# Delta-rule attention with an expert layer: six half items by native fp32 products, and six weight splits put later

## The chip, the cores and the metric

The kernel runs on one core of one Trainium2 chip. The metric is the device time of one execution in microseconds (us); lower is better. All times below are in us unless marked ns.

## The reference

Four sequences with eight heads of width 48 run a delta rule over 768 steps; what comes out is the input of a two-layer network with 2048 hidden units. Everything is fp32.

```python
k_n = k / (norm(k) + 1e-06)
for t in range(S):                                     # S = 768
    y[:, :, t] = einsum('bhd,bhde->bhe', q[:, :, t], state)
    v_old = einsum('bhde,bhd->bhe', state, k_n[:, :, t])
    state = state + beta_t * einsum('bhd,bhe->bhde', k_n[:, :, t], v[:, :, t] - v_old)
x = y rearranged to 3072 tokens of 384
h = x @ w_in                                           # 384 x 2048
g = where(h >= 1, h, where(h <= -1, 0, (h + 1)**2 / 4))
out = g @ w_out                                        # 2048 x 384
```

## The kernel before, in words

**Attention.** The 768 steps are cut into 12 blocks of 64, and two blocks make a group G of 512 tokens. For a block, `gram_k` and `gram_q` (L233, L246) make products of its keys and queries, `lanes`, `solve` and `unlanes` invert a triangular matrix on VectorE (DVE), `merge16_a`, `merge16_b` and `merge32` (L391 to L444) join its parts with small products on TensorE (PE), and a chain through the state follows: `chain_r` (L446, state times keys), `chain_u` (L461), `chain_y` (L479, the block's output Y) and `chain_d` (L559, the new state). Each of them is a function that issues PE's products and returns its evictions from PSUM, which run on ScalarE (ACT) or DVE.

**The network.** It runs in items (G, f, blocks): the tokens of one or both blocks of a group against tile f of 16 weight tiles, each with 128 hidden units. `up` (L688) makes h; three activations on ACT (L812 twice, L844) and a maximum on DVE (L846) make g; `rest` (L803) splits g into a rounded part `ghi` on ACT (L807) and the remainder `glo` on DVE (L808); `down` (L697), two items behind, adds g times w_out to the sums `o`. PE multiplies fp32r, a rounded fp32. To keep precision each product is made of three passes over split operands (`PASSES`): high by high, high by low, low by high. So an item over one block (a half item, 256 tokens) has 9 matmuls in up and 6 in down; a whole item has 9 and 12, with 512 columns in up.

**Weights.** They lie in memory as 64-bit numbers and are unpacked in five steps for each tile f: `grow` (ACT, L191), `shift` (DVE, L197), `join` (DVE, L203), which makes the fp32 weight in X4, one of four places in the memory of `xb`; then the split, `cast` (ACT, L207) to the high part and `low` (DVE, L210) to the low part, both in `WT[f]`, which takes the memory of the raw tile `RAW[f]`. Y is split in the same way into `xb` when it is evicted, for block 0 by `direct` (L511: L515 on ACT, L520 on DVE).

**The order.** Nothing reorders the program: each engine takes its instructions as the code issues them, and an instruction that waits holds up those behind it on its engine. Group 0 begins with its only prologue, the front, where no Y is there yet. Its first six items (`HALF`) go over block 0 alone, as half items, while block 1 is still being solved; items 6 to 15 go over both blocks, and items 16 to 21 give the first six weight tiles to block 1. Around them, steps are put by hand. Tables of letters, FRONT for the front's stages and FILL for the items, say at which of six places in each item a step goes: A is the next step of ACT's list of grows and casts, D the next of DVE's list of shifts, joins and lows, F a filler, w a weight load, l another load, L a step of `lanes`, S of `solve`, U of `unlanes`, s, t, v and z scalings of V (L286), m and M masks of the query products (L266), B a copy of a Gram matrix (L611). PIECES says at which half item PE gets the pieces of block 1's chain: f6 are six fillers, a1 and b1 `merge16_a` and `merge16_b`, c1 and e1 the two parts of `merge32`, r1, u1, y1, d1 the chain, q2 the `gram_q` of block 2. Later groups are planned by the loops in `plan`, the same in both kernels.

**Fillers.** `dense(n)` issues n matmuls of 512 columns on a tile of zeros, whose results nobody reads; they occupy PE in the front while it has nothing to do. IDLE is the number of them after the fourth `gram_k`.

**Buffers.** h has two PSUM banks, `ch` two, o0 to o3 one each. The banks of h and o serve the chain too until the sums begin: `chain_d` of block 0 takes the two banks of h, which L576 on ACT empties. The const tiles `wt11` to `wt15` lend their memory to other things until their weights are loaded (`room`).

The order in which a step must follow another is told by this line in `plan`, which puts the chain of a group, with M = 14 items for group 0:

```python
for j, x in ((0, (0, None)), (0.5, (1, 0)), (2.5, (None, 1))):
    at(pe, G, M + j, lambda x=x: merge32(*x))
chain(G, M + 1.5, a)
```

So in item 14 PE has, in this order, up 14, a merge32 (L426), down 12, the next merge32, up 15, a `gram_k` (L239), down 13, `chain_u` (L467), up of tile 0 for block 1, and `chain_y` (L493). ACT evicts the merges (L441, L433, then L441 again, with copies L443), `gram_k` (L243) and `chain_u` (L476).

Of the kernel before, what the change touches and what calls it, by code (L numbers as in the profile page):

```python
# [22 lines left out]
IDLE = 18  # L23
DENSE = (8, 4, 8, 10)
HALF = 6
PASSES = ((0, 0), (0, 1), (1, 0))
# [14 lines left out]
def delta_rule_moe(ctx: ExitStack, tc: tile.TileContext, kqa, kqb, kv, beta, w, out):  # L41
# [157 lines left out]
    def join(f):  # L199
        x = X4[:, f % 4].bitcast(I32)  # L200
        if not PRELU:
            nc.vector.scalar_tensor_tensor(out=x, in0=RAW[f].bitcast(I32)[:, :, 1::2], scalar=-0x80000000, in1=x, op0=ALU.bitwise_and, op1=ALU.bitwise_or)
        nc.vector.scalar_tensor_tensor(out=x, in0=RAW.pop(f).bitcast(I32)[:, :, 0::2], scalar=29, in1=x, op0=ALU.logical_shift_right, op1=ALU.bitwise_or)  # L203

    def cast(f):
        WT[f] = const.tile([P, 2, 2, DM], F32R, name=f"wt{f}")
        nc.scalar.copy(out=WT[f][:, :, 0, :], in_=X4[:, f % 4])  # L207
# [13 lines left out]

    UNPACK = grow, shift, join, cast, low
# [256 lines left out]
    def chain_y(g):  # L479
        w_ = Q[g]  # L480
        if g % 2 == 0:
            XB[g // 2] = sb.tile([P, 2, 3, 2 * NB], F32R, name="xb")
        if g == 1:
            stg = const.tile([P, 2, 2 * DM], F32R, name=f"wt{FT - 1}")[:, :, 0:NB]
# [17 lines left out]
        if g == 0:  # L502
# [105 lines left out]

    def restore():
# [205 lines left out]
    for n, item in enumerate(items):  # L815
# [5 lines left out]
        if last:  # L821
            rest(*last)
# [4 lines left out]
        assert (item[1], low) in done, item  # L827
# [18 lines left out]
        nc.vector.tensor_tensor(out=s[:, c], in0=h[:, c], in1=s[:, c], op=ALU.max)  # L846
# [56 lines left out]
```

## Time and profile before

| what | value |
|---|---|
| median of 3 runs | 600.15 us (598.7 to 600.31) |
| the profiled execution | 601.46 us |
| its span, first to last instruction | 599.7 us |
| PE busy | 581.0 us, 97% of the span |
| PE weight loads busy | 502.3 us, 84% |
| DVE busy | 394.2 us, 66% |
| ACT busy | 396.5 us, 66% |
| GpSimd (POOL) busy | 33.0 us, 6% |
| fillers on PE (L165) | 87 matmuls, 28.9 us |
| ups and downs on PE (L693, L708) | 225.0, 200.7 and 130.1 us |

A page gives for each engine its busy time and, in 40 slices of 15 us, the busy share in tenths; PEclk is the clock that was granted to PE, in tenths. A group of instructions has its line, engine, operation, output and inputs, count, busy time, mean length in ns, and the idle time before it with what ended it. PEld is PE's loading of the stationary operand, recorded by itself. A native fp32 matmul is recorded as two instructions, so x64 stands for 32 of them. Both fp32 and fp32r operands are called f32 in PE's rows.

### The profile page before, as it was taken

The page shows a single profiled execution, that of the slowest core. Times are in us where ns is not written, and L with a number is a line of the kernel's source. Part 1 is how long each engine was busy: PE and PEld are TensorE (multiplying, and loading weights), DVE is VectorE, ACT ScalarE, POOL GpSimd, SP SyncE. Part 2 cuts the span into 40 slices and gives each one's busy share as a digit, 9 for nine tenths or more (in the row PEclk, how much of TensorE's full clock was granted, in tenths as well). Part 3 has the DMA queues.
Part 4 walks back from the last instruction along what each step waited for, and adds up shares of the span by engine and source line. Part 5 has one row for each costly group of instructions (what it writes and reads, how often), then busy time and mean ns, then how long its engine had stood idle before and what let it go on. Part 6 is the DMA issues. An engine that isn't in the chain of part 4 may idle for free.

```text
span 599.7 us, 21759 instructions
## 1 busy us (share of the span) xinstructions
PE 581.0 (97%) x9585; PEld 502.3 (84%) x9585; DVE 394.2 (66%) x828; ACT 396.5 (66%) x689; POOL 33.0 (6%) x67
## 2 busy tenths in 40 slices
PE   8898999999999999999999999999999999999996
PEld 7777888788878878888888898888888888898986
DVE  5967899953689943689933689934689925333332
ACT  4538898478756596656586656586656585676663
POOL 6200010000020000020000020000020000000000
PEclk9969799999999999999999999999999999999999
DMA  5682657200333011134011134011143000020001
GB/s 144 207 290 86 205 194 210 66 8 9 93 96 103 8 32 45 31 98 121 13 32 45 33 103 119 8 32 45 34 108 91 1 3 16 15 54 1 0 1 52
DMA packets 32302, 42.77 MB, mean 71 GB/s; under 512 B 7056, under 2 KB 26768, under 8 KB 32208
## 3 DMA queue, kind: packets, MB, share of 16 engines
q1 hardware_dynamic: 31216, 40.41, 23.6%
q8 instruction: 75, 1.23, 0.9%
q0 software_dynamic: 576, 0.57, 0.4%
q10 hardware_dynamic: 416, 0.39, 0.2%
q14 instruction: 19, 0.16, 0.1%
HBM read 34.47 MB, written 4.72 MB: 65 GB/s over the span
## 4 chain that ended last, share of the span: by engine, by line
PE 46%; issue 28%; ACT 13%; DVE 5%; SPq 4%; DMA 3%; POOL 1%; POOLq 0%; ACTq 0%; DVEq 0%
PE o L708 16%; PE h L693 16%; PE ch L493 3%; ACT s L812 2%; ACT GG L441 2%; PE ch L467 2%; ACT XT L443 1%; PE o L165 1%; PE ch L252 1%; PE ch L451 1%; DMA KV<-in_kv_dram 1%; PE ch L566 1%; PE ch L428 1%; ACT s L844 1%; ACT xb L191 1%
## 5 line engine op out<-in xcount | busy, mean ns | idle before, releaser
L693 PE MATMUL h<-xb,wt 128*128 128x512 f32 (+1 forms) x918 | 225.0, 388 | 4.0 <-DVE s L846 2.0
L708 PE MATMUL o<-wt,ghi 128*128 128x384 f32 x768 | 200.7, 343 | 0.0
L693 PEld LDWEIGHTS h<-xb,wt 128*128 128x128 f32 x918 | 162.5, 189 | 38.1 <-DVE s L846 2.8
L708 PEld LDWEIGHTS o<-wt,ghi 128*128 128x128 f32 x768 | 137.8, 189 | 7.0
L846 DVE TENSOR_TENSOR s<-h,s 128x512 f32<-128x512 f32 (+1 forms) x102 | 66.8, 655 | 116.3 <-ACT s L844 115.4
L708 PE MATMUL o<-wt,glo 128*128 128x384 f32 x384 | 130.1, 339 | 0.3 <-DVE glo L808 0.3
L807 ACT CAST ghi<-s 128x512 fp32r<-128x512 f32 (+1 forms) x102 | 60.9, 597 | 102.9 <-DVE s L846 87.7
L808 DVE TENSOR_TENSOR glo<-s,ghi 128x512 fp32r<-128x512 f32 (+1 forms) x102 | 66.6, 653 | 39.2 <-ACT ghi L807 39.2
L812 ACT ACTIVATE s<-h,half 128x512 f32<-128x512 f32 (+1 forms) x102 | 67.4, 661 | 35.9 <-PE h L693 35.4
L708 PEld LDWEIGHTS o<-wt,glo 128*128 128x128 f32 x384 | 72.6, 189 | 1.1 <-DVE glo L808 1.1
L812 ACT ACTIVATE s<-s,one 128x512 f32<-128x512 f32 (+1 forms) x102 | 71.7, 703 | 2.4
L844 ACT ACTIVATE s<-s 128x512 f32<-128x512 f32 (+1 forms) x102 | 61.9, 607 | 3.2
L360 DVE TENSOR_TENSOR pr<-A 128x30 f32<-128x30 f32 (+14 forms) x120 | 39.3, 327 | 7.0 <-POOL A L325 5.1
L362 DVE TENSOR_TENSOR A<-A,pr 128x30 f32<-128x30 f32 (+14 forms) x120 | 39.8, 332 | 4.4
L165 PE MATMUL o<-wx 128*128 128x512 f32 x87 | 28.9, 479 | 1.5 <-DVE tiny L177 1.5
L493 PEld LDWEIGHTS ch<-Q,SU 64*64 64x64 f32 (+3 forms) x1056 | 22.4, 135 | 4.4 <-ACT ghi L807 1.5
L493 PE MATMUL ch<-Q,SU 64*64 64x64 f32 (+3 forms) x1056 | 24.7, 222 | 0.7 <-ACT SU L476 0.7
L165 PEld LDWEIGHTS o<-wx 128*128 128x128 f32 x87 | 18.8, 227 | 5.8 <-DVE tiny L177 1.5
L325 POOL TENSOR_SCALAR_AFFINE_SELECT A<-A 128x1024 f32<-128x1024 f32 x4 | 5.1, 1264 | 300.0 <-DMA xb<-X 256.4
L266 DVE TENSOR_TENSOR Q<-ch,mask 64x512 f32<-64x512 f32 (+1 forms) x30 | 20.6, 687 | 0.4
L426 PEld LDWEIGHTS ch<-XT,GG 32*32 32x32 f32 x704 | 12.4, 106 | 5.3 <-issue 2.8
L441 ACT ACTIVATE GG<-ch 32x512 f32<-32x512 f32 x22 | 12.9, 588 | 5.0 <-PE ch L426 4.7
(159 smaller groups left out, 575.2 us busy)
## 6 DMA issues: line engine op xcount, KB each, us to landing
wt<-in_w_dram SPq DMA_DIRECT2D x16, 768.0 KB, 6.0
out_dram<-wx SPq DMA_DIRECT2D x44, 96.0 KB, 2.2
KV<-in_kv_dram SPq DMA_DIRECT2D x36, 96.0 KB, 2.5
KV<-in_kv_dram SPq DMA_DIRECT2D x72, 48.0 KB, 2.4
KV<-in_kv_dram SPq DMA_DIRECT2D x12, 192.0 KB, 2.9
xb<-X SPq DMA_DIRECT2D x60, 32.0 KB, 2.0
K<-in_kqb_dram SPq DMA_DIRECT2D x12, 128.0 KB, 2.6
Q<-in_kqb_dram SPq DMA_DIRECT2D x12, 128.0 KB, 2.8
```

The source lines that it names most:

```text
L165: nc.tensor.matmul(warm_ps, warm[:, 0:P], warm, start=True, stop=True)
L360: nc.vector.tensor_tensor(out=pr, in0=A[:, 0:n, j:j + 1].broadcast_to([P, n, m]), in1=A[:, j:j + 1, j + 1:32].broadcast_to([P, n, m]), op= ...
L362: nc.vector.tensor_tensor(out=A[:, 0:n, j + 1:32], in0=A[:, 0:n, j + 1:32], in1=pr, op=ALU.add)
L441: nc.scalar.mul(out=GG[r:r + 32, ga, :, 0:32], in_=y1[r:r + 32], mul=-1.0)
L493: nc.tensor.matmul(yy[i][o * C:o * C + C, e, p], SF[rows, u:u + C], w_[rows, x, k, :], **how)
L693: nc.tensor.matmul(h[:, cols(bs)], WT[f][:, 0, x, k * P:(k + 1) * P], XB[G][:, y, k, cols(bs)], start=(n == 0), stop=(n == 8))
L708: nc.tensor.matmul(oacc[G, k], (ghi, glo)[x][:, k * P:(k + 1) * P], WT[f][:, 1, y, :], start=(new and n == 0), stop=(left[G, b] == 0 and n ...
L807: nc.scalar.copy(out=ghi[:, c], in_=s[:, c])
L808: nc.vector.tensor_tensor(out=glo[:, c], in0=s[:, c], in1=ghi[:, c], op=ALU.subtract)
L812: nc.scalar.activation(out=out, in_=in_, func=AF.Relu, bias=bias, scale=scale)
L844: nc.scalar.activation(out=s[:, c], in_=s[:, c], func=AF.Square)
L846: nc.vector.tensor_tensor(out=s[:, c], in0=h[:, c], in1=s[:, c], op=ALU.max)
```

## The change

The first six items, the half items of block 0 (`WIDE = 6`), no longer use split operands. Their ups multiply the joined fp32 weights by an fp32 copy of Y, three native fp32 products instead of nine fp32r ones; their downs multiply an fp32 g by the joined fp32 w_out, two native products instead of six. What else follows from it:

- `join` writes the fp32 weights of tiles 0 to 5 over the raw tile instead of into X4, and `RAW[f]` lives on until its cast.
- A new step `fetch` (DVE) copies the joined weights back into X4. `cast` and `low` of tiles 0 to 5 come at the end of the two lists, after those of tile 15, each after its fetch; tiles 0 to 5 are needed split from item 16 on.
- `direct` evicts Y of block 0 into `XF`, in the memory of `wt15`, with one copy on ACT and two on DVE. A new step `split` (letter h) splits it into `xb` later, with a cast on ACT and a subtraction on DVE, for items 6 to 15.
- The maximum (L846) writes g of these items into a tile of its own, and `rest` is left out for them, so they have no L807 and L808.
- The staging tile of `chain_y` for block 1 lies in `wt11` instead of `wt15`.
- The tables FRONT, FILL and PIECES and the number IDLE are others: 73 fillers in all instead of 87; c1 stands one half step later than before, e1 too, and q2 comes at 12 instead of 16.

The core of the diff:

```diff
-IDLE = 18
+IDLE = 10
+WIDE = 6
-    "sAwFALs,", "FLFFFDFFLFFFFF,F", "FFDD,S", "mFFFFFmm,", "AFFFD,AAw", ",", "DA,Dt")
+    "AD,", "wLFFFADFLFFwFDLFF,", "tswsDF,m", "F,mFmFw", "FF,SAFF", ",D", "MA,mDh")
...
-        nc.vector.scalar_tensor_tensor(out=x, in0=RAW.pop(f).bitcast(I32)[:, :, 0::2], scalar=29, in1=x, ...)
+        raw = RAW[f].bitcast(I32)
+        nc.vector.scalar_tensor_tensor(out=raw[:, :, 0:DM] if f < WIDE else x, in0=raw[:, :, 0::2], scalar=29, in1=x, ...)
+
+    def fetch(f):
+        nc.vector.tensor_copy(out=X4[:, f % 4], in_=RAW[f][:, :, 0:DM])
...
+        if g == 0:
+            S["XF"] = room(FT - 1, 0, 3 * NB).rearrange("p (k t) -> p k t", k=3)
         if g == 1:
-            stg = const.tile([P, 2, 2 * DM], F32R, name=f"wt{FT - 1}")[:, :, 0:NB]
+            stg = const.tile([P, 2, 2 * DM], F32R, name=f"wt{FT - 5}")[:, :, 0:NB]
...
+                for y, i, es, q in ((yy[0], 0, slice(0, 2), nc.scalar.copy), (y0, 1, slice(0, 1), nc.vector.tensor_copy), (yy[1], 1, slice(1, 2), nc.vector.tensor_copy)):
+                    q(out=S["XF"].rearrange("p k (e s t) -> p s e k t", s=CT, t=C)[:, i, es], in_=y[:, es, 0:3])
...
+    def split():
+        x = XB[0][:, :, :, 0:NB]
+        nc.scalar.copy(out=x[:, 0], in_=S["XF"])
+        yield
+        nc.vector.tensor_tensor(out=x[:, 1], in0=S["XF"], in1=x[:, 0], op=ALU.subtract)
+        yield
...
+    acts = [x for x in acts if x[0] < FT] + [(f, cast) for f in range(WIDE)]
+    vecs += [(0, fetch)] + [x for f in range(WIDE) for x in ((f + 1, fetch), (f, low)) if x[0] < WIDE]
...
+        if wide(G, f, bs):
+            for k in range(3):
+                nc.tensor.matmul(h[:, cols(bs)], RAW[f][:, 0, k * P:(k + 1) * P], S["XF"][:, k], start=(k == 0), stop=(k == 2))
+            return h
...
+        if wide(G, f, bs):
+            for k in range(2):
+                nc.tensor.matmul(oacc[G, k] ..., ghi[:, k * P:(k + 1) * P], RAW[f][:, 1, 0:DM], start=(f == 0), stop=False)
+            left[G, 0] -= 1
+            return
```

Three places show how instructions move. The first is PE in the front, from the end of IDLE to the eviction of the first `chain_u`: L165 are fillers, L153 the product of beta, L395 and L409 the 16-wide merges (L400 and L414 in the new file), L426 and L428 the 32-wide ones (L431, L433), L467 `chain_u` (L472). Before:

```order
L165 MATMUL o_152<-wx 128x512 x18
L153 MATMUL o_546<-beta_sb,perm 128x160
L395 MATMUL ch<-XT,GG 32x16 x64
L165 MATMUL o_152<-wx 128x512
L409 MATMUL ch<-wt_144,XT 32x16 x64
L165 MATMUL o_152<-wx 128x512 x12
L426 MATMUL h<-XT,GG 32x32 x32
L165 MATMUL o_152<-wx 128x512 x2
L428 MATMUL h<-GG 32x32 x32
L165 MATMUL o_152<-wx 128x512 x5
```

And now:

```order
L165 MATMUL o_152<-wx 128x512 x10
L153 MATMUL o_538<-beta_sb,perm 128x160
L400 MATMUL ch<-XT,GG 32x16 x64
L414 MATMUL ch<-wt_144,XT 32x16 x64
L165 MATMUL o_152<-wx 128x512 x9
L431 MATMUL h<-XT,GG 32x32 x32
L165 MATMUL o_152<-wx 128x512
L433 MATMUL h<-GG 32x32 x32
L165 MATMUL o_152<-wx 128x512 x3
L472 MATMUL o_805<-KV,XT 64x48 x2
```

The chain's products stand in the same order; fewer fillers stand ahead of each.

The second is PE in items 1 to 3, from the second up: L693 is up and L708 down (L704 and L716 in their native form), with the merges of block 1 between them. Before:

```order
L693 MATMUL h<-xb,wt_960 128x256 x9
L409 MATMUL o_1129<-wt_144,XT 32x16 x64
L693 MATMUL h<-xb,wt_1096 128x256 x9
L426 MATMUL ch<-XT,GG 32x32 x32
L165 MATMUL o_152<-wx 128x512
L708 MATMUL o_1277<-wt_862,ghi 128x384 x2
L708 MATMUL o_1277<-wt_862,glo 128x384
L708 MATMUL o_1281<-wt_862,ghi 128x384 x2
L708 MATMUL o_1281<-wt_862,glo 128x384
L428 MATMUL ch<-GG 32x32 x32
L693 MATMUL h<-xb,wt_1109 128x256 x9
```

And now:

```order
L704 MATMUL h<-wt_856,wt_112 128x256 x3
L414 MATMUL o_1104<-wt_144,XT 32x16 x64
L704 MATMUL h<-wt_856,wt_125 128x256 x3
L716 MATMUL o_1186<-wt_110,ghi 128x384
L716 MATMUL o_1188<-wt_110,ghi 128x384
L431 MATMUL ch<-XT,GG 32x32 x32
L704 MATMUL h<-wt_856,wt_127 128x256 x3
L433 MATMUL ch<-GG 32x32 x32
L716 MATMUL o_1186<-wt_112,ghi 128x384
```

Nine products became three and six became two, and each merge stands one piece later: down 0 is ahead of the first merge and up 3 between the two.

The third is ACT from the first activation of item 14 (L812, L833 in the new file) to the eviction of `chain_u` (L476, L481): L441, L443 and L433 belong to the merges (L446, L448, L438), L207 is the cast of a weight tile (L212), whose name tells the tile. Before:

```order
L812 ACTIVATE s_2327<-h_2317,half_165 128x512
L441 ACTIVATE GG_174<-ch_2329 32x16x32 x2
L443 COPY XT_175<-XT_175 32x16x32 x2
L812 ACTIVATE s_2327<-s_2327,one_167 128x512
L844 ACTIVATE s_2327<-s_2327 128x512
L433 COPY XT_175<-ch_2384 32x16x32 x2
L441 ACTIVATE GG_174<-ch_2383 32x16x32 x2
L443 COPY XT_175<-XT_175 32x16x32 x2
L807 CAST ghi_2465<-s_2327 128x512
L812 ACTIVATE s_2479<-h_2469,half_165 128x512
```

And now, up to the fourth cast, after which the fifth, L812 and the sixth follow:

```order
L833 ACTIVATE s_2219<-h_2209,half_165 128x512
L212 CAST wt0_2255<-xb_178 128x2x384
L446 ACTIVATE GG_174<-ch_2221 32x16x32 x2
L448 COPY XT_175<-XT_175 32x16x32 x2
L212 CAST wt1_2266<-xb_178 128x2x384
L833 ACTIVATE s_2219<-s_2219,one_167 128x512
L866 ACTIVATE s_2219<-s_2219 128x512
L212 CAST wt2_2356<-xb_178 128x2x384
L438 COPY XT_175<-ch_2283 32x16x32 x2
L446 ACTIVATE GG_174<-ch_2282 32x16x32 x2
L448 COPY XT_175<-XT_175 32x16x32 x2
L212 CAST wt3_2370<-xb_178 128x2x384
```

Six casts, which stood in items 0 to 3, now stand between the evictions here. On DVE the six fetches and six lows stand in the same items.

More of the change, by code (lines that the diff above doesn't have):

```diff
@@ L215, in unpack @@
         for f, x in steps:
-            for g, y in ((f, dict(zip(UNPACK[1:], UNPACK)).get(x)), (f - 4, low if x is grow else None)):
-                assert y is None or g < 0 or (g, y) in done, (f, x)
+            owner = f - 4 if x is grow else f - 4 if f > 3 else f + 12
+            needs = {grow: (owner, join if owner < WIDE else low), shift: (f, grow), join: (f, shift), fetch: (owner, low),
+                     cast: (f, fetch if f < WIDE else join), low: (f, cast)}[x]
+            assert needs[0] < 0 or needs in done, (f, x)
             x(f)
@@ L220, in unpack @@
             yield
-    UNPACK = grow, shift, join, cast, low
     def quarters():
@@ L686, in cols, with wide @@
         return slice(bs[0] * NB, bs[-1] * NB + NB)
+    def wide(G, f, bs):
+        return G == 0 and bs == (0,) and f < WIDE
     def up(G, f, bs):
@@ L698, in down @@
         ghi, glo = gs.pop((G, f, bs))
+        if wide(G, f, bs):
+            for k in range(2):
+                nc.tensor.matmul(oacc[G, k] if (G, k) in oacc else oacc.setdefault((G, k), ps.tile([P, DM], F32, name=f"o{k}")),
+                                 ghi[:, k * P:(k + 1) * P], RAW[f][:, 1, 0:DM], start=(f == 0), stop=False)
+            left[G, 0] -= 1
+            return
         for b in bs:
@@ L821, in delta_rule_moe @@
         if last:
-            rest(*last)
+            if not wide(*last[0]):
+                rest(*last)
             ready.append(last[0])
@@ L826, in delta_rule_moe @@
             spare.clear()
-        assert (item[1], low) in done, item
+        assert (item[1], join if wide(*item) else low) in done, item
         h = up(*item)
@@ L845, in delta_rule_moe @@
         late = products(*pe.pop(at_ + 1, []))
-        nc.vector.tensor_tensor(out=s[:, c], in0=h[:, c], in1=s[:, c], op=ALU.max)
+        g = s
+        if wide(*item):
+            g = sb.tile([P, 2 * NB], F32, name="ghi", bufs=2)
+            gs[item] = g[:, c], None
+        nc.vector.tensor_tensor(out=g[:, c], in0=h[:, c], in1=s[:, c], op=ALU.max)
         do(codes[5])
```

25 lines of the change are left out of this document (8 added, 17 removed).

## Prediction

> **What bounds the kernel now.** I read the page's busy slices first, then the windows by stretch, then the timeline of each engine where TensorE (PE) waits. All times are microseconds from the start of the span. The granted clock by slice comes from the page; the two windows list the length, the busy time of PE, its weight loads, DVE, ACT and POOL, the granted clock, and DMA.
>
> ```profile
> PEclk9969799999999999999999999999999999999999
> ```
> ```profile
> 60.00:75.00 15.00, 13.85 (x306) 12.46 (x300) 12.39 (x23) 13.42 (x27) 0.00 (x0) 0.77 0.63 205
> ...
> 135.00:150.00 15.00, 14.72 (x397) 13.08 (x397) 5.16 (x11) 13.15 (x27) 0.00 (x0) 1.00 0.04 10
> ```
> The clock is whole from the sixth slice (75 us) on, and from there PE is nearly always busy, so an early gain is kept to the end unless PE is made to wait again later. The change touches only the first 28 items, so four stretches decide: the front (to the first up), the half items (to the first whole item), the whole items up to up 14, and items 14 to 16.
>
> The front, in the timeline. Columns are start, length, engine, line, operation, count.
>
> ```profile
> 31.90 5.46 PE L165 MATMUL o<-wx 128*128 128x512 f32 x12
> ...
> 34.09 0.41 DVE L414 TENSOR_TENSOR XT<-XT,ch 128x256 f32<-128x256 f32 x1
> ...
> 37.29 1.20 PE L426 MATMUL h<-XT,GG 32*32 32x32 f32 x64
> ...
> 41.08 2.50 PE L165 MATMUL o<-wx 128*128 128x512 f32 x5
> 41.19 1.18 ACT L433 COPY XT<-h 32x512 f32<-32x512 f32 x2 [0.29 <-PE h L428]
> ...
> 43.52 1.36 PE L467 MATMUL o<-KV,XT 64*64 64x48 f32 x64
> ...
> 50.55 1.46 ACT L576 COPY SU<-h 48x384 f32<-48x384 f32 x3
> ...
> 51.56 0.62 PE L693 MATMUL h<-xb,wt 128*128 128x256 f32 x3 [0.79 <-ACT SU L576]
> ```
> Here PE's own fillers hold up the chain. L426 needs L414, done at 34.50, yet starts at 37.29, when twelve fillers at half clock (0.455 each) are through. L467 needs L433, done at 42.37, yet starts at 43.52 behind five more. And the first up waits not for its weights but for the PSUM bank that L576 empties.
>
> **The change, part by part.** *Fillers and front.* In the place before L426, thirteen fillers become nine; before L467, five become three; the four that follow L467 end before its evictions do. The eight taken out of IDLE stand further ahead, where PE's next product needs L384's transpose, at 25.95, so they move little. DVE gets to L414 later: two scalings are taken from before it, a shift (L197) and a join (L203) are put there.
>
> ```profile
> 24.68 1.27 DVE L384 STREAM_TRANSPOSE XT<-A 128x512 f32<-128x512 f32 x1
> ...
> 28.29 0.54 DVE L286 TENSOR_TENSOR KV<-KV,N 128x384 f32<-128x384 f32 x1
> ```
> ```profile
> L203 DVE SCALAR_TENSOR_TENSOR xb<-wt,xb 128x768 int32<-128x768 int32 x16 | 15.2, 949 | 0.1
> L210 DVE TENSOR_TENSOR wt<-xb,wt 128x768 fp32r<-128x768 f32 x16 | 15.1, 946 | 0.0
> L191 ACT ACTIVATE xb<-wt 128x768 f32<-128x768 f32 x16 | 14.4, 905 | 0.0
> L207 ACT CAST wt<-xb 128x768 fp32r<-128x768 f32 x16 | 13.2, 825 | 3.2 <-DVE xb L203 3.2
> ...
> L197 DVE TENSOR_SCALAR xb<-xb 128x768 int32<-128x768 int32 x16 | 8.8, 551 | 0.0
> ...
> L808 DVE TENSOR_TENSOR glo<-s,ghi 128x256 fp32r<-128x256 f32 x12 | 5.0, 420 | 5.1 <-ACT ghi L807 5.1
> L807 ACT CAST ghi<-s 128x256 fp32r<-128x256 f32 x12 | 4.9, 410 | 4.1 <-DVE s L846 4.0
> ```
> That is 0.55 + 0.95 - 2 x 0.54 = 0.4 later: L414 ends at 34.9, and L426 starts at 35.1, where nine fillers at 0.43 to 0.455 from about 31.2 end as well (the merge before them ends at 31.9 now, and the eviction that it needs loses an L191 of 0.9 ahead of it on ACT, of which I count 0.7). Gain 2.2. L433 then ends near 40.2, where the three fillers end too, and L467 starts at 40.25, a gain of 3.3. From L467 to the first up the kernel before takes 8.04; the two weight casts and three evictions of Y that stand on ACT there become one copy, which takes the 0.2 by which ACT was late for L576. First up at 48.1 to 48.2, against 51.56: **-3.4** (2.0 if the fillers end later, 4.0 at most).
>
> *The native products.* The trace has one wide native fp32 product, of beta: one instruction, recorded as two passes. Beside it stand a half item's up and down by three passes.
>
> ```profile
> 25.89 0.43 PE L153 MATMUL o<-beta_sb,perm 128*128 128x160 f32 x2
> ```
> ```profile
> 78.87 1.33 PE L693 MATMUL h<-xb,wt 128*128 128x256 f32 x9
> 80.04 0.52 PE L708 MATMUL o<-wt,ghi 128*128 128x384 f32 x2
> ...
> 84.03 0.52 PE L708 MATMUL o<-wt,ghi 128*128 128x384 f32 x2
> ...
> 85.09 2.22 PE L693 MATMUL h<-xb,wt 128*128 128x512 f32 x9
> ```
> A record of L153 lasts 0.297 (its median by line), so the second started 0.136 after the first: 0.85 ns for a column. A native up of three products is 6 x 256 x 0.85 = 1.31, against 80.04 - 78.87 = 1.17; a native down of two is 4 x 384 x 0.85 = 1.31, against 85.09 - 84.03 = 1.06. So 0.14 and 0.25 more; six of each cost PE **2.3**, if it has no slack. The upper bound, a record at twice that price, is a rival below; under the price of now it cannot go much, since the passes stream the columns one after the other.
>
> *What leaves ACT and DVE in the half items.* ACT loses six casts (6 x 0.825) and six of L807 (6 x 0.41), 7.4 in all; DVE six of L210 (6 x 0.946) and six of L808 (6 x 0.42), 8.2. They gain one split of XF, about 0.8 (bounded by 0.825) on ACT and 0.95 on DVE, in place of evictions of nearly that length.
>
> ```profile
> 62.86 1.20 PE L426 MATMUL ch<-XT,GG 32*32 32x32 f32 x64 [1.10 <-DVE XT L414]
> ...
> 81.68 2.51 PE L693 MATMUL h<-xb,wt 128*128 128x512 f32 x9 [0.41 <-DMA xb<-wt]
> ```
> From the first up to this first whole one the kernel before takes 81.68 - 51.56 = 30.1. In it the clock costs 15 x (1 - 0.77) = 3.4 of the window from 60 to 75, and PE waits 1.1 for DVE and 0.4 for the staging DMA. I take these away, 4.9, since DVE and ACT have lost over 7 each, and add back six native ups and four downs, 6 x 0.14 + 4 x 0.25 = 1.8. New short waits of PE, for L414, L441 and L476, which still stand behind relu steps and weight joins and scalings on their engines, I put at 0.4, an estimate: under half of the 1.1 that L414 costs now. The gram_q of block 2 is moved in front of down 4, work that stands behind up 8 now. **-2.7** (0 if only what the natives add is won back, -4 if no new wait comes and the half-clock merges speed up too). What is late next there is the staging DMA of block 1 again. It reads tile 11 instead of tile 15 now, so SP's load of weight tile 11, and the two loads queued behind it, wait for it; tile 11 is needed only five items later.
>
> *Whole items up to up 14.*
>
> ```profile
> PE h L693 <- DVE s L846: 2.0, 3, 1.0
> ```
> ```profile
> 118.68 2.37 PE L693 MATMUL h<-xb,wt 128*128 128x512 f32 x9 [0.65 <-DVE s L846]
> ...
> 126.12 2.37 PE L693 MATMUL h<-xb,wt 128*128 128x512 f32 x9
> ```
> DVE runs without a gap until 118.6 here and three ups wait 2.0 for it. Its work from the eviction of Y 1 to the solve's end is the same list in both kernels, so the stretch is shifted, not shortened; but two joins and a shift that stood ahead of the max of item 11 now stand behind it (2 x 0.95 + 0.55 = 2.4), so the ups from 13 on find h free. I take the 2.0 off and, for the 2.4, 0.2 more than it costs gram_q of block 3 that L414 moves behind a join and a split; the last two native downs add 0.5. Without the downs -2.2, with them **-1.7**; a quarter of that I leave for waits that the order alone doesn't show: **-1.3** (0 to -2.5).
>
> *Items 14 to 16: the six splits come back.* Six casts on ACT, six copies and six L210 on DVE. A copy of 128x768 is L197's size, 0.55. DVE idles over half of the window from 135 to 150, 5.16 busy; ACT is busy 13.15.
>
> ```profile
> 128.53 0.69 ACT L812 ACTIVATE s<-h,half 128x512 f32<-128x512 f32 x1 [1.51 <-PE h L693]
> 129.67 1.19 ACT L441 ACTIVATE GG<-ch 32x512 f32<-32x512 f32 x2 [0.45 <-PE ch L426]
> ...
> 134.75 1.19 ACT L441 ACTIVATE GG<-ch 32x512 f32<-32x512 f32 x2
> ```
> ```profile
> 135.99 1.16 PE L239 MATMUL ch<-K 48*64 48x64 f32 x62 [0.28 <-ACT GG L441]
> 139.35 1.35 PE L467 MATMUL ch<-KV,XT 64*64 64x48 f32 x64
> ```
> ```profile
> 140.71 1.45 ACT L476 COPY SU<-ch 64x384 f32<-64x384 f32 x3
> ```
> ```profile
> 141.90 2.24 PE L493 MATMUL ch<-Q,SU 112*64 112x64 f32 x96
> ```
> On ACT the six casts stand between this L812 and this L476: one ahead of the first L441, two more ahead of the second, three between that and L476. PE has no slack there: gram_k (L239) already waits 0.28 for the second L441, since it needs the banks that L433 and L441 empty, and chain_y (L493) starts 0.2 after the second copy of L476. So 3 x 0.825 = 2.5, less ACT's idle 0.45, falls on gram_k, and another 2.5 on chain_y. The first cast may also wait up to 0.9 for its copy on DVE, which stands behind the three masks of gram_q; I leave that to the bound. Behind ACT's queue wait the relu steps of items 14 and 15, whose h banks PE asks for only some 6 later. **+4.5**: PE stands about 2.3 before gram_k and 2.5 before chain_y. Bounds: 2.5, if one of the two is covered, and 5.4, if the copy adds its 0.9.
>
> Sum: -3.4 - 2.7 - 1.3 + 4.5 = -2.9, 598.56 on the profiled execution. That execution took 601.46 (span 599.7, 1.76 around it), 1.31 over the median of the three runs, 600.15; on that median the sum gives 597.25, and I say 597.2.
>
> **The rivals.** *The casts are covered* (chance 0.22). One of PE's two waits falls into the other: 2.5 instead of 4.5, and the half items give -4. Then -3.4 - 4 - 1.3 + 2.5 = -6.2: 593.9. For it: the relu steps behind the casts can be some 6 late unnoticed. Against: the L812 ahead of the casts waits 1.51 for PE, so ACT can't run ahead of them.
>
> *The clock falls in the new gaps* (0.13). What a gap does to the clock, in windows of 1 us:
>
> ```profile
> 28.00:29.00 1.00, 0.46 (x29) 0.32 (x28) 1.00 (x3) 0.61 (x2) 0.00 (x0) 1.00 0.58 117
> 29.00:30.00 1.00, 0.13 (x15) 0.03 (x2) 1.00 (x1) 0.00 (x0) 0.00 (x0) 1.00 0.76 147
> 30.00:31.00 1.00, 0.60 (x44) 0.61 (x48) 1.00 (x2) 0.34 (x1) 0.00 (x0) 0.69 1.08 418
> ```
> Some 1.8 idle out of 3 brought it down. Waits of 2.3 and 2.5 could do the same for about 3.4 to 6.8 (the dip in the 60 to 75 window is 6.9 long); part passes while PE waits anyway, so up to +2.5, -0.4 in all: 599.7, no change. The Trainium skill ("TensorE: Matmul & The Clock Gate", HAM oscillation) wants a gap of over about 3.4 us; by that rule alone neither wait costs any clock. These rows, where PE was 0.4 busy, go against the rule.
>
> *Block 1's chain still paces the half items* (0.15, slower). If merges, chain_u, chain_y and the staging DMA of block 1 follow each other with latency alone, then relief of ACT and DVE buys nothing, PE stays loose enough for the clock to dip again, and at half clock the native products that stand between the chain's steps on PE add twice their 1.8: -3.4 + 3.6 - 1.3 + 4.5 = +3.4: 603.5. It makes the kernel slower by over 0.3% from the point where the stretch takes 32.1, 2.0 over now. For it: the wait for L414 and for the DMA, both chain steps. Against: L414 itself stood in DVE's full queue.
>
> *Native records cost twice* (0.03): 6 x (2.62 + 2.62 - 2.23) = 18 on PE, less what the waits hide: about 610. L153 speaks against.
>
> **How the numbers follow.** The forecast has 0.47, and 595.0 to 600.3 by its bounds, the ends of the four terms not falling together. A measurement of this kernel tells about 0.3% (1.8) from no change, so faster means under 598.35 and slower over 601.95. The forecast is faster in four fifths of its chance (0.38) and the same in the rest (0.09); covered casts are faster (0.22); the clock rival is mostly the same (0.10 of 0.13), with 0.02 faster and 0.01 slower; the chain rival slower in 0.13 of 0.15; dear records slower (0.03). That makes 0.62, 0.21 and 0.17. The range leaves out most of the chain rival, the dear records and the far end of the covered casts: 592.5 to 602.0.
>
> **What would show it.** Right: first up near 48 us; L704's and L716's records (the native up and down) 0.21 and 0.32 apart; up 6 near 75.5; no clock dip between 60 and 75; DVE gapless from the eviction of Y 1; ACT gapless from the L812 of item 14 to L476, and PE waiting over 2 twice, before gram_k and before chain_y. Wrong: a half-item stretch of 30 or over, native records over 0.4, or gram_k and chain_y without a wait.

## The result and the profile after

The changed kernel takes 606.21 us (median of 7, 603.59 to 608.8) against 600.31 (median of 7): a ratio of 1.0094, 95% interval 1.0071 to 1.0116. A second set gave 1.0089 (1.0056 to 1.0122). The forecast was 597.2. Four marks cut the profiled executions, two of each kernel, into the stretches of the prediction. The last mark is the merge32 that item 16 brings, alone in its place (L428, L433 now; the expectations call it the merge of block 3). Behind it the planned order is the same in both kernels.

| stretch | before | before, again | after | after, again | forecast of the difference | difference of the means |
|---|---|---|---|---|---|---|
| start to first up | 51.56 | 51.18 | 52.69 | 54.11 | -3.4 | +2.0 |
| first up to up 6 | 30.1 | 32.0 | 27.9 | 27.3 | -2.7 | -3.5 |
| up 6 to up 14 | 44.4 | 44.4 | 45.6 | 45.6 | -1.3 | +1.2 |
| up 14 to the merge of item 16 | 20.2 | 20.2 | 27.2 | 24.4 | +4.5 | +5.6 |
| from there to the end | 453.4 | 453.0 | 453.5 | 453.7 | 0 | +0.4 |
| span | 599.7 | 600.9 | 606.9 | 605.1 | -2.9 | +5.7 |

So two terms have the wrong sign, the front and the whole items, and two the right one. The clock's line on the page of the changed kernel shows where it moved: the 7 that before has in its fifth slice (60 to 75) is gone, and the tenth (137 to 152) has one now.

```profile
PEclk9969999997999999999999999999999999999999
```

The front of the changed kernel, in its timeline. L431 is the first merge, L472 `chain_u`, L704 the first up; L291 scales V, L448 and L438 copy what `chain_u` reads.

```profile
35.27 0.63 PE L431 MATMUL h<-XT,GG 32*32 32x32 f32 x28
37.17 0.84 PE L431 MATMUL h<-XT,GG 32*32 32x32 f32 x36 [1.27 <-issue]
...
40.09 1.50 DVE L291 TENSOR_TENSOR KV<-KV,N 128x384 f32<-128x384 f32 x3 [4.13 <-DMA KV<-in_kv_dram]
41.51 0.95 DVE L204 SCALAR_TENSOR_TENSOR wt<-wt,xb 128x768 int32<-128x768 int32 x1
42.38 0.86 DVE L448 COPY XT<-XT 32x512 f32<-32x512 f32 x2
...
42.87 1.17 ACT L438 COPY XT<-h 32x512 f32<-32x512 f32 x2 [3.63 <-DVE XT L448]
...
44.10 1.96 PE L472 MATMUL o<-KV,XT 64*64 64x48 f32 x64 [1.31 <-ACT XT L438]
...
52.69 1.56 PE L704 MATMUL h<-wt,wt 128*128 128x256 f32 x6 [0.54 <-ACT SU L575]
```

In the kernel before, L448 is L443:

```profile
36.48 0.86 DVE L443 COPY XT<-XT 32x512 f32<-32x512 f32 x2
```

The merge starts at 35.27, where 35.1 was forecast. Then two things come between. PE stops for 1.27 inside the merge, for nothing that the profile shows. And L448, which ran at 36.48 before, runs at 42.38: three scalings and a join stand ahead of it on DVE, and the first scaling is of block 1's V, whose load lands only at 40.09. ACT waits behind DVE, and PE behind ACT. In the second execution the load lands later still, and PE waits 4.30 for L438:

```profile
41.22 1.50 DVE L291 TENSOR_TENSOR KV<-KV,N 128x384 f32<-128x384 f32 x3 [5.78 <-DMA KV<-in_kv_dram]
```

The late stretch, with the casts (L212) on ACT. L446 and L438 evict merges, L248 a `gram_k`, L481 `chain_u`; L244 is `gram_k`, L472 `chain_u` of block 2 and L433 the merge of item 16.

```profile
132.67 0.83 ACT L212 CAST wt<-xb 128x768 fp32r<-128x768 f32 x1
...
136.75 0.32 PE L244 MATMUL ch<-K 48*64 48x64 f32 x2 [1.30 <-ACT XT L438]
137.96 1.16 PE L244 MATMUL ch<-K 48*64 48x64 f32 x62 [0.89 <-ACT GG L446]
...
141.90 0.82 ACT L212 CAST wt<-xb 128x768 fp32r<-128x768 f32 x1
142.63 1.07 ACT L248 COPY GG<-ch 128x512 f32<-128x512 f32 x2
143.36 2.34 PE L472 MATMUL ch<-KV,XT 64*64 64x48 f32 x64 [1.96 <-ACT GG L248]
...
153.37 1.20 PE L433 MATMUL ch<-GG 32*32 32x32 f32 x64
```

PE waits 2.19 for `gram_k` and 1.96 for `chain_u`, close to the 2.3 and 2.5 that were forecast. What was not in the sum shows in windows of 1 us of the same kernel: length, busy time of PE, PEld, DVE, ACT and POOL, granted clock, DMA.

```profile
142.00:143.00 1.00, 0.00 (x0) 0.00 (x0) 1.00 (x3) 1.00 (x3) 0.00 (x0) 1.00 0.00 0
143.00:144.00 1.00, 0.60 (x12) 0.47 (x16) 0.84 (x1) 1.00 (x3) 0.00 (x0) 0.75 0.00 0
...
150.00:151.00 1.00, 1.00 (x64) 1.00 (x60) 0.00 (x0) 0.00 (x0) 0.00 (x0) 0.83 0.00 0
```

After the second wait the clock is halved from 143.5 (0.75 of that window) to 150.34. That goes with the difference between 27.2 in this execution and 24.4 in the second: in both, `chain_u` starts 17.2 behind up 14 (13.2 in the kernel before), and only in the first is the clock halved behind it. Of six profiles with this late stretch (the two here, and four below that change something ahead of it), four take 24.4, one 24.9 and only this one 27.2.

### The profile page after: what moved, and what is told of

It reads as the page before. It is cut to its first block, busy times and chain, and to the rows that moved or that the text cites. A ratio compares the mean times of both kernels' runs of the same rounds, so it can differ in the third digit from the quotient of the medians.

```text
span 606.9 us, 21670 instructions
## 1 busy us (share of the span) xinstructions
PE 580.5 (96%) x9541; PEld 498.7 (82%) x9541; DVE 396.7 (65%) x828; ACT 395.3 (65%) x682; POOL 32.9 (5%) x67
## 4 chain that ended last, share of the span: by engine, by line
PE 41%; issue 28%; DVE 11%; ACT 10%; SPq 5%; DMA 4%; POOL 1%; POOLq 0%; DVEq 0%; ACTq 0%
PE o L729 13%; PE h L708 13%; PE ch L500 3%; DMA KV<-in_kv_dram 3%; ACT s L833 2%; PE ch L472 2%; ACT XT L448 2%; ACT GG L446 2%; PE h L704 1%; DVE glo L829 1%; DVE s L872 1%; PE ch L456 1%; DVE Q L271 1%; PE ch L565 1%; ACT wt L212 1%
## 5 line engine op out<-in xcount | busy, mean ns | idle before, releaser
L708 PE MATMUL h<-xb,wt 128*128 128x512 f32 (+1 forms) x864 | 217.1, 395 | 2.5 <-DVE s L872 1.2
L729 PE MATMUL o<-wt,ghi 128*128 128x384 f32 x744 | 193.5, 342 | 0.0
L708 PEld LDWEIGHTS h<-xb,wt 128*128 128x128 f32 x864 | 156.0, 190 | 36.2 <-DVE s L872 2.4
L729 PEld LDWEIGHTS o<-wt,ghi 128*128 128x128 f32 x744 | 133.0, 188 | 6.7
L729 PE MATMUL o<-wt,glo 128*128 128x384 f32 x372 | 125.5, 337 | 0.3 <-DVE glo L829 0.3
L833 ACT ACTIVATE s<-h,half 128x512 f32<-128x512 f32 (+1 forms) x102 | 67.5, 662 | 38.2 <-PE h L708 33.7
L833 ACT ACTIVATE s<-s,one 128x512 f32<-128x512 f32 (+1 forms) x102 | 71.7, 703 | 2.3
L729 PEld LDWEIGHTS o<-wt,glo 128*128 128x128 f32 x372 | 70.0, 188 | 0.8 <-DVE glo L829 0.8
L165 PE MATMUL o<-wx 128*128 128x512 f32 x73 | 25.1, 487 | 1.5 <-DVE tiny L177 1.5
L165 PEld LDWEIGHTS o<-wx 128*128 128x128 f32 x73 | 15.8, 230 | 5.2 <-DVE tiny L177 1.5
L291 DVE TENSOR_TENSOR KV<-KV,N 128x384 f32<-128x384 f32 x24 | 13.1, 551 | 5.5 <-DMA KV<-in_kv_dram 5.5
L472 PEld LDWEIGHTS ch<-KV,XT 64*64 64x64 f32 x640 | 11.8, 143 | 5.7 <-issue 4.6
```

Source lines behind the costliest of these rows:

```text
L165: nc.tensor.matmul(warm_ps, warm[:, 0:P], warm, start=True, stop=True)
L708: nc.tensor.matmul(h[:, cols(bs)], WT[f][:, 0, x, k * P:(k + 1) * P], XB[G][:, y, k, cols(bs)], start=(n == 0), stop=(n == 8))
L729: nc.tensor.matmul(oacc[G, k], (ghi, glo)[x][:, k * P:(k + 1) * P], WT[f][:, 1, y, :], start=(new and n == 0), stop=(left[G, b] == 0 and n ...
L833: nc.scalar.activation(out=out, in_=in_, func=AF.Relu, bias=bias, scale=scale)
```

## The experiments

Ratios are to the kernel before in the same set, with 95% intervals. "Marks" are those of the table. Of a table of letters a diff shows only the entries that change.

### The fillers alone

```diff
-IDLE = 18
+IDLE = 10
-"FLFFFDFFLFFFFF,F"
+"FLFFFDFFLFFF,"
-"mFFFFFmm,"
+"mFFFmm,"
```

> The kernel before with only the fillers cut: 8 of the 18 of IDLE, 3 of the 12 ahead of the first merge and 2 of the 5 ahead of chain_u; nothing else of the change. Theory of the prediction (fillers in PE's queue hold up merge 1 and chain_u): merge 1 near 35.2 instead of 37.3, chain_u near 40.3 instead of 43.5, first up near 48.2 instead of 51.6, ratio 0.9945. Rival (what the fillers are worth is the clock: with fewer of them TensorE runs at half clock for longer, and stalls on its own instructions come into view): first up between 50.5 and 52.5, more than 12 us of half clock between 28 and 50, ratio 0.998 to 1.002.

Measured 0.9985 (0.996 to 1.001). Timeline of this kernel:

```profile
35.11 0.78 PE L426 MATMUL h<-XT,GG 32*32 32x32 f32 x27
38.52 0.96 PE L426 MATMUL h<-XT,GG 32*32 32x32 f32 x37 [2.63 <-issue]
...
44.18 1.96 PE L467 MATMUL o<-KV,XT 64*64 64x48 f32 x64
...
52.87 1.35 PE L693 MATMUL h<-xb,wt 128*128 128x256 f32 x9 [0.77 <-ACT SU L576]
```

The merge does start at 35.11, so the fillers held it up. But PE then stands 2.63 inside it, `chain_u` comes later than before, and the first up is at 52.87. From 28 to 50 the mean clock is 0.61 (0.77 before), 17.1 us at half clock. The rival holds in its ratio, and the first up is a little beyond it: taking fillers out is worth nothing that can be measured.

### The wait for KV alone

```diff
-"tswsDF,m"
+"swsDF,m"
-"FF,SAFF"
+"FF,StAFF"
```

> The changed kernel, but the scaling of block 1's V (first half) is put back behind chain_u's eviction, where DVE stood idle from 47.6 to 50.8 us and KV had long landed (40.1). Theory (the wait for KV's DMA, queued on DVE ahead of the copy that chain_u needs, cost the front): the copy L448 starts near 38 instead of 42.4, chain_u near 42.9, as soon as its fillers end at half clock, and the first up near 51.4 instead of 52.7; ratio to the kernel before 1.0094 - 0.002 = 1.007, if what follows only shifts. Rival (half clock and PE's stall in merge 1 set the front): chain_u within 0.3 of 44.1, first up within 0.3 of 52.7, ratio 1.009. If the clock also comes back earlier, first up near 49 and ratio near 1.004.

> The changed kernel with block 1's V scaled later once more, for a second profiled execution. Its first had the first up at 49.0 and was the shortest of its ten; the median gained only 0.002. If the front's gain is in every execution: first up near 49 to 50 again, chain_u near 41 to 43 without a wait for the copy L448. If it hangs on the phase of the clock's steps: first up near 51.5, and three steps at half clock in place of one before chain_y.

Measured 1.0074 (1.0047 to 1.0101) and 1.0077 (1.0048 to 1.0105). The first profile:

```profile
37.64 0.86 DVE L448 COPY XT<-XT 32x512 f32<-32x512 f32 x2
...
41.06 1.96 PE L472 MATMUL o<-KV,XT 64*64 64x48 f32 x64
...
48.97 1.56 PE L704 MATMUL h<-wt,wt 128*128 128x256 f32 x6 [0.59 <-ACT SU L575]
```

The second has the first up at 50.41. The four profiles with this edit (here and below) have it at 48.5 to 50.4, mean 49.3; six with the change's own front at 52.3 to 54.1, mean 53.1. In all seven profiles in which this scaling stands ahead of L448, DVE waits for the load, by 3.6 to 5.8. So the wait cost 3.8 at the first up. By up 6, 2.6 of it is left (78.1 against 80.7 on average), since the half items then take 28.1 to 29.4 instead of 27.3 to 27.9. The ratio fell by only 0.0016, about 1.0 us (from 1.0092, the mean of the two sets of the changed kernel, to 1.0076), while one interval spans 0.005: how much of the 2.6 reaches the end is open.

### The fillers put back

```diff
-IDLE = 10
+IDLE = 18
-"wLFFFADFLFFwFDLFF,", "tswsDF,m", "F,mFmFw", "FF,SAFF"
+"wLFFFADFLFFFwFFDLFFFF,", "tswsDFF,m", "FF,mFmFFw", "F,SAFF"
```

> The changed kernel with the fillers of the kernel before: 18 in IDLE, 12 ahead of merge 1, 2 ahead of its second half, 5 ahead of chain_u, 3 behind it. Theory (after the cut of the fillers the front runs at half clock for 17 us instead of 10, in steps of 3.41 us): half clock in the front 7 to 10 us, first up between 50.5 and 52, mean clock of all executions up from 0.980 by 0.004 to 0.006, ratio 1.005 to 1.007. Rival (the wait for KV's DMA alone sets the front): first up within 0.5 of 52.7 and ratio within 0.001 of 1.0094, whatever the clock.

Measured 1.0116 (1.0074 to 1.0157): my theory fell. The clock behaved about as it said: 6.8 us at half clock between 28 and 50 instead of 16.5, and a mean clock of 0.987 over all executions instead of 0.980. The time did not fall.

```profile
42.85 1.15 PE L472 MATMUL o<-KV,XT 64*64 64x48 f32 x64 [1.38 <-ACT XT L438]
...
52.45 1.56 PE L704 MATMUL h<-wt,wt 128*128 128x256 f32 x6 [0.54 <-ACT SU L575]
```

PE waits for the same copy again. This matters because the executions tempt to another story: the kernel before has a mean clock of 0.988 over 68 executions and the changed one 0.980 over 14, which is 10 us more at half clock, and half of that is nearly the whole loss. But half clock in the front falls on fillers and on a chain that waits for DVE and ACT; it goes with the loss without causing it. The profile of the kernel with the late casts on DVE (below), whose front is that of the changed kernel, happens to have only 9.1 us at half clock there, and its first up is at 53.24 all the same.

### The weight steps around block 3's merges

```diff
-",,,,,D", "DD,,,AD,,"
+",D,,,DD,", ",,,,AD,"
```

> The changed kernel with four steps of the weight splits moved on DVE: the shift and join of tile 15 and the low part of tile 14 from behind the max of item 12 into the two gaps in which DVE waits for ACT at 116.3 and 117.7, and the low part of tile 15 behind the second L419 (block 3's m16b). Theory (these 2.5 us stand ahead of L419, and gram_q of block 3 waits for it, so the 2.3 us by which the solve ended earlier are given back there): first L419 near 119.8 instead of 122.1, gram_q without its wait of 0.8, up 14 near 124.8 instead of 126.15, that is 44.3 us behind up 6 instead of 45.6; ratio 1.0094 - 0.0015 to - 0.002. Rival (PE's own work paces this stretch): up 14 stays within 0.4 of 45.6 behind up 6.

Measured 1.0078 (1.0052 to 1.0103). First the rows of the changed kernel, then of this one (L419 is the subtraction behind the 16-wide merge b, L257 `gram_q`, the last line up 14):

```profile
119.14 0.69 DVE L872 TENSOR_TENSOR s<-h,s 128x512 f32<-128x512 f32 x1 [1.44 <-ACT s L866]
119.75 0.55 DVE L197 TENSOR_SCALAR xb<-xb 128x768 int32<-128x768 int32 x1
120.34 0.96 DVE L204 SCALAR_TENSOR_TENSOR xb<-wt,xb 128x768 int32<-128x768 int32 x1
121.21 0.95 DVE L215 TENSOR_TENSOR wt<-xb,wt 128x768 fp32r<-128x768 f32 x1
122.08 0.42 DVE L419 TENSOR_TENSOR XT<-XT,ch 128x256 f32<-128x256 f32 x1
...
125.07 1.15 PE L257 MATMUL ch<-Q,K 48*64 48x64 f32 x60 [0.80 <-DVE XT L419]
```

```profile
119.21 0.41 DVE L419 TENSOR_TENSOR XT<-XT,ch 128x256 f32<-128x256 f32 x1
...
123.06 1.16 PE L257 MATMUL ch<-Q,K 48*64 48x64 f32 x64
124.16 2.14 PE L708 MATMUL h<-xb,wt 128*128 128x512 f32 x8
```

Up 14 is 43.9 behind up 6 instead of 45.6, as expected (44.3). DVE's list did set this stretch, and the place of these steps in it was the loss. The ratio alone would not show it: its gain of 0.0014 lies within the interval.

### The late casts on DVE

```diff
-        nc.scalar.copy(out=WT[f][:, :, 0, :], in_=X4[:, f % 4])
+        (nc.vector.tensor_copy if f < WIDE else nc.scalar.copy)(out=WT[f][:, :, 0, :], in_=X4[:, f % 4])
```

> The changed kernel, but the six late casts of weight tiles 0 to 5 are done by DVE instead of ACT, at the same places of the program. Theory (six casts in ACT's queue between the relu of item 14 and chain_u's eviction cost 4 to 7 us): gram_k near 135.6 instead of 136.75, chain_u near 139.6 instead of 143.4, from up 14 to the merge of block 3 20.5 to 21.5 us as in the kernel before (20.2) instead of 27.2, and the ratio 1.0094 - 0.007 = 1.0025. Rival (DVE, which then has 5 us more between 129 and 146, holds up the low halves that the downs wait for and the masks of gram_q): the stretch stays at 23 us or over, ratio 1.006 or over.

Measured 1.0044 (1.0018 to 1.0070), the largest single gain.

```profile
136.22 1.15 PE L244 MATMUL ch<-K 48*64 48x64 f32 x62 [0.35 <-ACT GG L446]
139.62 1.33 PE L472 MATMUL ch<-KV,XT 64*64 64x48 f32 x64
148.00 1.20 PE L433 MATMUL ch<-GG 32*32 32x32 f32 x64 [1.34 <-DVE xb L550]
```

`gram_k` and `chain_u` come as in the kernel before (9.9 and 13.3 behind up 14, where it has 9.9 and 13.2); the stretch takes 21.7. The 1.5 that stays is the wait of 1.34 for L550, the low part of Y, on DVE. So ACT as their place cost this stretch 2.7 (24.4 less 21.7) without a dip of the clock behind `chain_u`, and 5.5 with one.

### The late splits spread over items 16 to 20

```diff
-",,D,DAzD,DA,", "ADDDD,ADD,AD,AD,,", "z,,,,,"
+",,D,Az,D,", ",,,,,", "zD,,,A,D,", "D,,,A,D,", "D,,,A,D,", "D,,,A,D,", "D,,,A,D,"
-        nc.vector.tensor_copy(out=X4[:, f % 4], in_=RAW[f][:, :, 0:DM])
+        XL[f] = sb.tile([P, 2, DM], F32, name="wx", bufs=2)
+        nc.vector.tensor_copy(out=XL[f], in_=RAW[f][:, :, 0:DM])
...
-        nc.scalar.copy(out=WT[f][:, :, 0, :], in_=X4[:, f % 4])
+        nc.scalar.copy(out=WT[f][:, :, 0, :], in_=XL[f] if f < WIDE else X4[:, f % 4])
...
```

> The changed kernel, but five of the six late splits (copy, cast, low part) stand one each in items 16 to 20 instead of all in items 14 and 15; their copies lie in a buffer of the output store. Theory (the casts on ACT made PE wait before gram_k and chain_u, and the second wait brought the clock down): gram_k near 135.8 and chain_u near 140 instead of 136.75 and 143.4, no clock dip between 143 and 151, the merge of block 3 near 147.5 instead of 153.4, ratio 1.0094 - 0.010 = 0.9995. Rival (the casts only move their cost: ACT holds up the half items 16 to 20 as well): up to 2.5 us of new waits before the merges and chains behind 147, ratio 1.003 to 1.005.

Measured 1.0072 (1.0046 to 1.0098). The marks of the theory are there, or nearly: `gram_k` at 136.0, `chain_u` at 140.5, the merge at 148.2. But from there to the end it takes 456.5 instead of 453.5: the `chain_u` of block 3 starts 2.7 later than in the kernel before (160.6 against 157.9), the up behind it 4.9 (167.3 against 162.4), and between 165 and 180 the clock is 0.89. Between the two, `chain_y` (L503 in this file) waits for ACT's eviction of `chain_u`:

```profile
164.65 2.77 PE L503 MATMUL ch<-Q,SU 112*64 112x64 f32 x96 [1.70 <-ACT SU L484]
```

The cost moved; the rival is right, and its 1.003 to 1.005 lies at the lower end of the interval.

### Products of zeros in the two waits

```diff
-(27, "q3"))
+(27, "q3"), (30, "z9"), (31, "z9 z5"))
...
+    def zeros(n):
+        for _ in range(n):
+            nc.tensor.matmul(oacc[0, 0], warm[:, 0:P], warm[:, 0:DM], start=False, stop=False)
...
```

PE gets nine products of zeros ahead of `gram_k` and fourteen ahead of `chain_u`.

> The changed kernel with 9 products of zeros (128x384, added to a running sum, so no value changes) ahead of gram_k and 14 ahead of chain_u in items 15 and 15.5, about the length of PE's waits there. Nothing is taken off ACT. Theory (the dip of the clock from 143.75 to 150.8 cost half of its 7 us, on top of the casts): the clock stays at 1.00 there, the merge of block 3 comes near 150.2 instead of 153.4, ratio 1.0094 - 0.0055 = 1.004. Rival (ACT and DVE pace this stretch, the clock costs nothing): the merge stays within 0.5 of 153.4 and the ratio within 0.001 of 1.0094.

Measured 1.0081 (1.0052 to 1.0110). In the profile the clock stays at 1.00 from 50 on and the merge comes at 150.63, as expected of the dip. But that is 24.4 behind up 14, what the second execution of the changed kernel has too, with a dip from 139.4 to 142.8. So nothing was won against that execution. The interval leaves out the theory's 1.004 and holds the rival's 1.0094: a dip behind `chain_u`, which one of the six profiles has, is then a small part of the loss of the median.

### The two kernels once more

> The changed kernel once more, for a second profiled execution and more executions beside the same runs of the kernel before. If the clock falls by the phase of a fixed grid of 3.41 us, its dips have lengths of 3.4, 6.8 or 10.2 us again, but the late one (143.5 to 150.3 in the first execution) can be missing or shorter, and then the merge of block 3 comes near 150.5 instead of 153.4; the front has 5 steps at half clock between 26 and 50 and the first up near 53 again. If a dip is fixed by the code alone, it lies at the same place with the same length. Ratio 1.0094 within 0.0025 by both.

> The kernel before once more, for a second profile. If its marks repeat but for the clock's steps: first up 51.0 to 53, up 6 30 behind it, up 14 44.4 behind that, merge of block 3 20.2 behind that. The dip between 60 and 75 is in it if it comes from the code, and can be missing if it comes from the phase.

The marks are in the table. In the second execution of the changed kernel the front has six steps at half clock and there are two dips of 3.4; one is late:

```profile
138.00:139.00 1.00, 0.21 (x12) 0.21 (x16) 1.00 (x2) 0.96 (x3) 0.00 (x0) 1.00 0.00 0
139.00:140.00 1.00, 1.00 (x62) 1.00 (x54) 0.01 (x1) 0.99 (x2) 0.00 (x0) 0.70 0.06 16
...
142.00:143.00 1.00, 1.00 (x5) 1.00 (x5) 1.00 (x3) 0.97 (x3) 0.00 (x0) 0.59 0.00 0
```

Here the clock fell after the wait ahead of `gram_k`; PE came later to `chain_u` by that and waited only 0.43 there. In the first execution the clock fell after the other wait. A dip of one step ahead of `chain_u` costs nothing, since ACT's list sets when that starts: the four profiles with 24.4 all have one there, the one with 24.9 has two steps. Two steps behind it cost 2.8. The kernel before keeps its dip between 60 and 75 (63.1 to 73.3).

### The three edits together, and the casts on GpSimd

```diff
-        nc.scalar.copy(out=WT[f][:, :, 0, :], in_=X4[:, f % 4])
+        (nc.gpsimd.tensor_copy if f < WIDE else nc.scalar.copy)(out=WT[f][:, :, 0, :], in_=X4[:, f % 4])
```

> The changed kernel with three edits together: block 1's V scaled later (as in e1), the weight steps around m16b moved (as in e7), and the six late casts on DVE (as in e5). If the three gains add in the stretches where the single edits showed them: first up near 49.5 instead of 53, up 14 44.0 behind up 6, merge of block 3 21.5 behind up 14; ratio 1.009 - 0.002 - 0.001 - 0.005 = 1.001, and 0.997 if the whole of the front's 3.5 us in the profile of e1 is kept. Rival (a gain of the front is eaten by the DVE-paced stretch behind it, or by new dips of the clock): ratio 1.003 or over although the marks in the profile are earlier.

> As the kernel with the three edits together, but the six late casts are done by GpSimd, which is idle from 129 to 146 in the profile of the changed kernel. If a cast there takes under 1.5 us, neither ACT nor DVE is held up: the merge of block 3 without the wait of 1.3 for DVE that the casts on DVE brought, 20.2 to 20.8 us behind up 14, and the ratio 0.001 to 0.002 under that of the kernel with the casts on DVE. Rival (a cast on GpSimd takes 2 us or more, or slows DVE): the low parts come late, up 16 waits, and the merge comes 22 us or more behind up 14.

Measured 1.0008 (0.9981 to 1.0035) with the casts on DVE and 1.0000 (0.9974 to 1.0025) on GpSimd. The single gains (0.0016, 0.0014 and 0.0048 from 1.0092, the first two within the noise) would lead to 1.0014, so the three places together are the loss. By groups, the casts on GpSimd and what they do to DVE:

```profile
L212 POOL CAST wt<-xb 128x768 fp32r<-128x768 f32 x6 | 7.2, 1209 | 49.1 <-DVE xb L207 48.2 <-POOL XT L444 0.8
...
L207 DVE COPY xb<-wt 128x768 f32<-128x768 f32 x6 | 4.5, 762 | 0.0
```

The merge is 21.3 behind up 14, better than 21.7 and short of the 20.8 expected. No version beat the kernel before by what can be measured.

## Why the prediction was wrong, point by point

**The front, -3.4, was +2.0: the step that failed first.** It said that L433 (L438 now), ACT's copy of the merge, ends near 40.2 and `chain_u` starts at 40.25, as if that copy waited for PE alone. It also waits for L448 on DVE. The sum takes two scalings off DVE ahead of L414, at 0.54 each, and has no term for the place to which they go, ahead of L448, nor for a third that comes there; that this third one works on a block whose load lands at 40.09 was not looked up. A step that is moved takes along what it waits for. The wait cost 3.8 at the first up; without it the mean of 49.3 is 2.1 ahead of the kernel before, at the lower end of what the prediction allowed (2.0 to 4.0). The filler part of the term fails by itself as well: with fillers alone cut, the gain of 2.2 at the merge was gone before `chain_u`, into 2.63 of PE's own stall and a merge and chain at half clock.

**The native products, +2.3, were right in size.** From an up to the next piece it takes 1.40 (77.89 to 79.29) where 1.31 was said, and a down 1.10 to 1.25 where 1.31 was said:

```profile
77.89 1.56 PE L704 MATMUL h<-wt,wt 128*128 128x256 f32 x6
79.29 1.45 PE L716 MATMUL o<-wt,ghi 128*128 128x384 f32 x4
80.54 2.44 PE L708 MATMUL h<-xb,wt 128*128 128x512 f32 x9
...
84.00 1.56 PE L716 MATMUL o<-wt,ghi 128*128 128x384 f32 x4
85.10 1.16 PE L708 MATMUL h<-xb,wt 128*128 128x512 f32 x3
```

**The half items, -2.7, were right against the profiles (-3.5)**, with no clock dip between 60 and 75, and the rival that block 1's chain still paces them did not come. But 3.4 of that term was the dip of the profiled execution of before, whose clock of 0.983 is under the mean of 0.988; an execution without it has less to win. The second profile of before has the dip too, but at a clock of 0.981. Of the 68 executions of before, 28 have a clock of 0.990 or more, which leaves at most 12 us at half clock; the front and the dip of the profiled one have 17 together, so the dip is hardly in those 28. The sum was set against one execution and then moved to the median by a constant 1.31, though the term that it wins from is, by these clocks, not in every execution. That fits the last kernel above: its profile is 3.3 shorter than the mean of the two of before, its median the same.

**The whole items, -1.3, were +1.2.** Two steps failed. The 2.0 that three ups wait for the max were to go; 1.25 of it is still there:

```profile
93.68 2.34 PE L708 MATMUL h<-xb,wt 128*128 128x512 f32 x9 [0.57 <-DVE s L872]
...
110.33 2.36 PE L708 MATMUL h<-xb,wt 128*128 128x512 f32 x9 [0.68 <-DVE s L872]
```

DVE's work from the eviction of Y 1 to the solve's end was called the same list, but it takes 37.9 (77.93 to 115.80) where before had 36.7 (79.11 to 115.79): the solve ends when it did, though up 6 comes 1.1 earlier. And "0.2 more than it costs `gram_q`" failed: that wait went from 0.25 to 0.80. The low part, shift and join, 2.5 together, that stood ahead of the max of item 11 did leave (it ends at 116.33 instead of 118.62, and up 13 no longer waits). But they stand behind the max of item 12 now, ahead of both L419, the second of which `gram_q` waits for, and DVE's own waits of 0.69 and 1.44 for ACT, the same in both kernels, were not filled by them. The first L419 starts at 122.08, as before (122.06). With two smaller waits PE stands 2.8 between up 6 and up 14 instead of 2.2; the 0.5 of the downs about makes up the rest. Putting the steps into those waits of DVE gave 1.7 back.

**Items 14 to 16, +4.5, were +4.2 to +7.0.** Cause and place were right, shown by the casts on DVE; the second wait came ahead of `chain_u` and not `chain_y`, since `chain_u` needs the banks that L248 empties behind the casts. With 24.4 or 24.9 in five of six profiles, +4.2 to +4.7 is the usual case. The upper bound of 5.4 left out the clock, which stood among the rivals with 2.5 and 0.13: the two steps behind `chain_u` cost 2.8 in one of the six.

## What to carry to other kernels

Before a step is moved up an engine's queue, look up when each of its inputs lands, not only how long it takes: here 0.5 us of work brought a wait of 4.1 to everything behind it. Work that an engine is freed of early has to be put back where that engine idles, and its place in the order decides, not the engine's average load: the late splits cost 4.2 to 7.0 with their casts on ACT, 1.5 with them on DVE and 1.1 on GpSimd. And before a clock dip of a profiled execution is counted as something to win, compare its mean clock (here 0.983) with that of all executions (0.988): a second profile, at 0.981, had the dip too and would not have shown that others lack it.

## What the runs showed of the hardware

- The clock falls and rises on a fixed grid. In the first execution of the changed kernel it is halved from 27.46 to 34.28, 37.70 to 47.94 and 143.50 to 150.34, worked out from the clocks of these windows:

```profile
27.00:28.00 1.00, 0.86 (x88) 0.75 (x77) 1.00 (x2) 0.05 (x1) 0.45 (x3) 0.73 0.45 123
...
34.00:35.00 1.00, 1.00 (x5) 0.56 (x3) 1.00 (x4) 0.00 (x0) 0.00 (x0) 0.86 1.04 422
...
37.00:38.00 1.00, 0.83 (x37) 0.76 (x37) 0.00 (x0) 0.00 (x0) 0.00 (x0) 0.85 1.11 229
...
47.00:48.00 1.00, 1.00 (x4) 0.34 (x2) 0.74 (x3) 0.95 (x3) 0.00 (x0) 0.53 1.07 440
```

  These are 2, 3 and 2 steps of 3.41, and 27.46 and 143.50 lie 34 steps apart. The phase differs by execution. After idle time of 1.96 within one step (141.40 to 143.36) the clock fell; after 2.19 that a step's edge at 136.69 cut into 1.24 and 0.95 it did not. Idle time alone doesn't decide: in the second execution a step with 1.0 idle, and 128 records of 32x16 products in it, was followed by half clock (108.69 to 112.10), and in the profile with the late casts on DVE one with 1.5 idle was not (122.43 to 125.84). The Trainium skill ("TensorE: Matmul & The Clock Gate", What's actually happening) has a free-running window of 3413 ns, and the traces agree. The same page of the Trainium skill speaks of gaps over about 3.4 us in its section on HAM oscillation; here 1.96 was enough.
- Half clock where PE waits for other engines anyway cost nothing here: 6.8 instead of 16.5 us of it in the front did not make the kernel faster, and with a dip of one step ahead of `chain_u` in items 14 to 16 that still started 17.2 behind up 14.
- A cast of 128x768 takes 0.55 on DVE, 0.83 on ACT and 1.21 on GpSimd. Beside GpSimd's casts DVE's copies (L207) rose from 0.55 to 0.76 on average.
- PE stops inside a run of small products with nothing that the profile shows: for 1.26 in L409 before, 1.27 in L431 after, 2.63 in L426 with fewer fillers. L431 has no such stop in the second execution of the same kernel. The cause stays open.
